# Loading x of the fourth batch at the start into a fourth buffer, instead of after slot 0 into the first batch's buffer

## The chip, the cores and the metric

The kernel runs on one core of one Trainium2 chip, which has eight. The core has five engines that work through instruction streams of their own: TensorE (PE; its weight loads are listed as PEld), VectorE (DVE), ScalarE (ACT), GpSimd (POOL) and SyncE (SP). Here SP issues nearly all plain transfers, POOL the indirect ones (gathers and scatters of rows by a list of indices), and sixteen DMA engines move the bytes. The metric is the device time of one execution in microseconds (us); lower is better. All inputs and outputs lie in the chip's HBM, in float32.

## What is computed

A small attention with a state of 32 rows per head comes first, and its output goes through two mixture-of-experts layers with the best expert per token (the first has a capacity per expert).

```python
# x (4, 8, 512, 64), state (4, 8, 32, 64): batch, head, token or state row, width
a     = softmax(x @ state^T / 8);   xread = a  @ state     # over the 32 state rows
a2    = softmax(state @ x^T / 8);   sread = a2 @ x         # over the 512 tokens
t     = concat([xread, sread], tokens)                     # 2304 rows of 512
for w_gate, w1, w2, capacity in (layer 0, layer 1):        # 8 experts, 512 -> 1024 -> 512
    e, gate = argmax, softmax value of t @ w_gate
    t = gate * (relu(t @ w1[e]) @ w2[e])                   # layer 0: rows over capacity give 0
```

## The kernel before, in words

The order of instructions on every engine is written out by hand (a manual schedule); only the semaphores decide when each starts. Each engine works strictly in that order.

**Attention.** The four batches are four "slots" (`slot(b)`, L850). One batch of x is a tile `xb` of 128 partitions by 8 heads, 4 token groups and 64 columns, 1 MiB in all (8 KiB per partition). `xload(b, n)` (L714) takes a buffer of the tag `xb` and issues the load in n pieces on SP's queue. The tag has three buffers, so batch 3 takes the buffer of batch 0. Batches 0, 1 and 2 are loaded at the start (L721 to L723); batch 3 is loaded at the end of slot 0, through the list `late` that `slot` runs last (L914, L974).

Slot b works on three batches at a time. For batch b+2 it turns x (`front_T`, L768: eight PE transposes `pt<-ident,xb` at L775 for the first half, eight for the second, each copied by ACT into `xt`), and makes the scores (`front_S`, L784). For batch b+1 it does both softmaxes (`soft_max`, `soft_exp1`, `soft_exp2`, `soft_sum1`, `soft_end`; DVE, ACT and POOL). For batch b it makes the reads: `av` (L859, tile `pav`, stored to the HBM tensor `xrows` by SP at L861) and the state's reads `sr` (L868, `pt<-xb,e2n`, the last use of that batch's `xb`; DVE takes it over at L869 as `ysr`). On PE a slot runs: `back_T` (L847), `av(0)`, `front_T` first half, `av(2)`, `sr`, `av(1)`, `front_T` second half, the state rows' turn (L588), `av(3)`, and so on. In slot 1, `front_T` reads batch 3.

**Routing beside it.** From slot 1 on, `tick` places pieces of the routing of finished batches between the others: DVE works out each token's expert (L281 to L376), PE adds up counts (L629, L630 with `upper` and `ones`, from the tile `rs` that DVE writes at L618 to L624), and `enlist` builds the experts' row lists (L333, L335 on DVE, L341 on PE). In slot 1 the counts of batch 0 give the expert with which the first layer starts (`popular`); SP then loads its weights (`load_first`, L703 and L270, tile `raw`), and POOL gathers its first 512 rows (`gather_early`, L559, into `ysb`).

**Layers.** After slot 3, PE turns the gathered rows (L1012) and the first layer begins (L1045 for the first product, L1055 for the second, in three passes of split float32). Stages of up to 512 rows of one expert follow until the end.

The three lines that decide where x of batch 3 goes and when it is loaded are

```python
t = ap_.tile([P, H, R, D], F32, tag="xb", name="xb", bufs=3)          # L715
for f in late: f()                                                    # L914, end of slot(b)
slot(0, TICKS[0], steps(0), late=(lambda: xload(3, 2),))              # L974
```

Of the kernel before, what the change touches and what calls it, by code (L numbers as in the profile page):

```python
# [10 lines left out]
F32 = mybir.dt.float32  # L11
# [9 lines left out]
P = 128  # L21
B, H, S, D = 4, 8, 512, 64
# [6 lines left out]
R = S // P  # L29
# [25 lines left out]
TICKS = ((0, 0, 0, 0, 0, 0, 0), (4, 4, 4, 4, 4, 4, 4), (6, 6, 6, 6, 6, 6, 6), (4, 4, 4, 4, 4, 4, 4))  # L55
# [22 lines left out]
def moe_kernel(ctx: ExitStack, tc: tile.TileContext, x, state, wg1, w1a, w2a, cap, wg2, w1b, w2b, out):  # L78
# [21 lines left out]
    def bc(ap, shape):  # L100
        return ap.to_broadcast(shape)
# [5 lines left out]
    def tick(n=1):  # L107
        clock[0] += 1
        while n > 0 and bgq:
            try:  # L110
                if next(bgq[0]) is PAUSE:
                    break
                n -= 1
            except StopIteration:
                bgq.popleft()
# [592 lines left out]
    with ExitStack() as ac:  # L708
        ap_ = ac.enter_context(tc.tile_pool(name="attn", bufs=1))
# [2 lines left out]
        xb_ = {}  # L712

        def xload(b, n):  # L714
            t = ap_.tile([P, H, R, D], F32, tag="xb", name="xb", bufs=3)  # L715
            k = H // n
            for a in range(n):
                SP.dma_start(out=t[:, a * k:(a + 1) * k], in_=x[b, a * k:(a + 1) * k].rearrange("h (p r) d -> p h r d", p=P))
            xb_[b] = t

        xload(0, 4)  # L721
        xload(1, 2)
        xload(2, 2)  # L723
        SP.dma_start(out=cap_i, in_=bc(cap.bitcast(I32).rearrange("(o c) -> o c", o=1), [P, 2]))
        SP.dma_start(out=wg2q[:, :, 0:E], in_=wg2.rearrange("(c p) e -> p c e", p=P))

        sd = ap_.tile([P, B, NH, P], F32, name="sd")
        vg = ap_.tile([P, B, NH, GW], F32, name="vg")
# [4 lines left out]
        def pt():  # L733

            if banks:
                banks.rotate(-1)
                return banks[0]()
            return ps.tile([P, 512], F32, tag="pt", name="pt", bufs=2)
# [29 lines left out]
        def front_T(n, i):  # L768

            if i == 0:  # L770
                xt_[n] = ap_.tile([P, H, 2, P], F32, tag="xt", name="xt")
            p = pt()
            for j in range(2):
                for q in range(2):
                    PE.transpose(p[:, (2 * j + q) * P:(2 * j + q + 1) * P], xb_[n][:, 2 * i + j, 2 * q:2 * q + 2, :].rearrange("p r d -> p (r d)"), ident)  # L775
            ACT.copy(xt_[n][:, 2 * i:2 * i + 2].rearrange("p h q c -> p (h q c)"), p)
# [10 lines left out]
        def soft_max(n, style=0):  # L787

            nb = ap_.tile([P, NH], F32, tag="nb", name="nb")
            s2 = ap_.tile([P, NH], F32, tag="s2", name="s2")  # L790
            u = [ap_.tile([P, S // NS, NS], F32, tag=f"u{o}", name=f"u{o}") for o in range(2)]
            m1 = [ap_.tile([P, S // NS], F32, tag=f"m1{o}", name=f"m1{o}") for o in range(2)]
            e2_[n] = ap_.tile([P, NH, 2, 2 * P], F32, tag="e2T", name="e2T", bufs=2)
            e1_[n] = ap_.tile([P, 2, NH, 2, P], F32, tag="e1T", name="e1T", bufs=2)
            r2_[n] = ap_.tile([P, NH], F32, tag="r2", name="r2", bufs=2)
            sm_[n] = nb, s2, u, m1

            def col_max():
                DVE.tensor_reduce(out=nb, in_=psT.rearrange("p o (a c) -> p a o c", a=NH), axis=AX.XY, op=ALU.max)
                tick(TK[0])  # L800
                DVE.tensor_scalar(nb, nb, -0.125, None, op0=ALU.mult)

            if not style:
                col_max()
            for o in range(2):
                DVE.transpose(u[o].rearrange("p k s -> p (k s)"), psT[:, o])
                tick(TK[0])
                DVE.tensor_reduce(out=m1[o], in_=u[o], axis=AX.X, op=ALU.max)
                tick(TK[0])
                POOL.tensor_tensor(out=u[o], in0=u[o], in1=bc(m1[o][:, :, None], [P, S // NS, NS]), op=ALU.subtract)  # L810
            if style:
                col_max()

        def soft_exp2(n):
            nb, s2, u, m1 = sm_[n]
            for a in range(NH):
                ACT.activation(out=e2_[n][:, a], in_=psT[:, :, a * 256:(a + 1) * 256], func=AF.Exp, bias=nb[:, a:a + 1], scale=0.125, accum_out=s2[:, a:a + 1])

        def soft_exp1(n, o):
            nb, s2, u, m1 = sm_[n]  # L820
            ACT.activation(out=u[o], in_=u[o], func=AF.Exp, scale=0.125)

        def soft_sum1(n, o):
            nb, s2, u, m1 = sm_[n]
            DVE.tensor_reduce(out=m1[o], in_=u[o], axis=AX.X, op=ALU.add)
            tick(TK[1])
            DVE.tensor_scalar(m1[o], m1[o], 1e-9, None, op0=ALU.add)
            tick(TK[1])
            DVE.reciprocal(out=m1[o], in_=m1[o])  # L829
            POOL.tensor_tensor(out=u[o], in0=u[o], in1=bc(m1[o][:, :, None], [P, S // NS, NS]), op=ALU.mult)  # L830
# [11 lines left out]
        def back_T(b, e2n, q):  # L842

            p = pt()
            for r in range(2):
                for a in range(NH):
                    PE.transpose(p[:, r * 256 + a * P:r * 256 + (a + 1) * P], e2_[b][:, a, r, q // 2 * P:(q // 2 + 1) * P], ident)  # L847
            ACT.copy(e2n[:, q:q + 2, :].rearrange("p r c -> p (r c)"), p)

        def slot(b, ticks, work=None, late=()):  # L850

            n, m = b + 1, b + 2
            nn, mm = n < B, m < B

            def av(r):

                pv = psT if not nn and r in (1, 2) else pav
                for a in range(NH):
                    PE.matmul(pv[:, a, 0:GW], e1_[b][:, r % 2, a, r // 2], vg[:, b, a], start=True, stop=True)  # L859
                ACT.copy(xr[:, r], pv[:, :, 0:GW])  # L860
                SP.dma_start(out=xrows[b * ST:b * ST + S, 0:DM].rearrange("(p r) (a w) -> p r a w", p=P, a=NH)[:, r], in_=xr[:, r, :, 0:HH * D])  # L861

            def sr():
                psr = pt()
                for a in range(NH):
                    for q in range(R):
                        for h in range(HH):
                            PE.matmul(psr[NS * h:NS * (h + 1), a * D:(a + 1) * D], e2n[:, q, a * P + NS * h:a * P + NS * (h + 1)], xb_[b][:, a * HH + h, q, :], start=(q == 0), stop=(q == R - 1))  # L868
                DVE.tensor_tensor(out=ysr[b % 2].rearrange("p (a d) -> p a d", a=NH), in0=psr[:, 0:NH * D].rearrange("p (a d) -> p a d", a=NH), in1=bc(r2_[b][:, :, None], [P, NH, D]), op=ALU.mult)  # L869

            def beside(i):
                for f in (work or {}).get(i, ()):
                    f()
                tick(ticks[i])

            e2n = ap_.tile([P, R, NH * P], F32, tag="e2n", name="e2n")
            if nn:
                soft_max(n, 1)
            back_T(b, e2n, 0)
            back_T(b, e2n, 2)  # L880
            beside(0)
            av(0)
            if mm:
                front_T(m, 0)
                front_T(m, 1)
            beside(1)
            av(2)
            if nn:
                soft_exp1(n, 0)
                soft_exp1(n, 1)  # L890
                soft_exp2(n)
            sr()
            beside(2)
            if nn:
                soft_sum1(n, 0)
            av(1)
            if mm:
                front_T(m, 2)
                front_T(m, 3)
            beside(3)  # L900
            if nn:
                soft_sum1(n, 1)
                soft_sum2(n)
            av(3)
            DVE.tensor_tensor(out=lgs[:, b, 0:R], in0=xr[:, :, 0, HH * D:GW], in1=xr[:, :, 1, HH * D:GW], op=ALU.add)
            beside(4)
            if nn:
                soft_end(n, 0)
                soft_end(n, 1)
            beside(5)  # L910
            if mm:
                front_S(m)
            beside(6)
            for f in late:  # L914
                f()

        warm(WARM)
        with tc.tile_pool(name="start", bufs=1, space=bass.MemoryType.PSUM) as sp:
# [45 lines left out]
        def steps(b, *more):  # L964

            w = {}
            for i, f in tuple(zip(READ, reads[b])) + more:
                w.setdefault(i, []).append(f)
            return w
# [1 line left out]
        def more(b):  # L971
            return tuple((i, lambda c=c: wsplit(0, c)) for c, (k, i) in enumerate(SPLIT0) if k == b)

        slot(0, TICKS[0], steps(0), late=(lambda: xload(3, 2),))  # L974
        bgq += [route(0, 1, chain(popular(rp, 0), load_first(0, (0,)))), set_apart(rp, 0), enlist_batch(0)]
        slot(1, TICKS[1], steps(1))
        bgq += [early_list(rp, 0), named("early", gather_early()), load_first(0, (1,)), route(1, 1)]
# [575 lines left out]
```

## Time and profile before

| | |
|---|---|
| time, median of 3 runs | 474.64 us (471.83 to 475.17) |
| the profiled execution | 473.61 us, of which the span from first to last instruction is 471.8 us |
| PE busy in the span | 425.9 us (90%) |
| DVE, ACT, POOL busy | 187.6, 165.4, 199.6 us (40%, 35%, 42%) |
| moved by DMA | 89.19 MB, 189 GB/s on average |
| mean granted TensorE clock | 0.975 of full speed |

The profiled execution is 1.03 us below the median of the three timed runs. Attention fills roughly the first 80 us of the span, where all engines take turns; after that PE is busy nearly without a break. A share of the whole span therefore says little about a change in the attention part: there the waits in a stretch of a few microseconds count, and whether what they delay reaches PE's long stretch behind them.

### The profile page before, as it was taken

To read this page: it belongs to the slowest core of one execution; us is meant where nothing else is said; L and a number is where in the kernel's file an instruction comes from. 1 tells how busy PE (TensorE), PEld (TensorE's weight loads), DVE (VectorE), ACT (ScalarE), POOL (GpSimd) and SP (SyncE) were. 2 spreads that over 40 slices of the span, in tenths; PEclk is the share of its full clock that TensorE was granted. 3 is DMA by queue.
4 is the path that set the end of the run, shared out by engine and by line. 5 is a ranking of instruction groups with operands and counts; after the bars stand their busy time and mean duration, and the time that the engine had idled before them with its cause. 6 is when DMAs were issued, how large, how long until landed. Compare 5 with 4: busy or idle time off the path is not lost. (4 is left out here: it accounts for less than half of the span.)

```text
span 471.8 us, 8130 instructions
## 1 busy us (share of the span) xinstructions
PE 425.9 (90%) x2757; PEld 308.2 (65%) x2757; DVE 187.6 (40%) x655; ACT 165.4 (35%) x288; POOL 199.6 (42%) x175
## 2 busy tenths in 40 slices
PE   7869577969999989999998899999989999999991
PEld 5647365757874775685775587778746856758780
DVE  7985755797140243141164141971420101411011
ACT  3757355220244421335521346203522213452110
POOL 6441264221704527305344435558443404777003
PEclk9998879998999999999999999999999999999997
DMA  7262739994999976907933300119998858210002
GB/s 234 85 167 92 222 97 297 230 172 176 394 360 385 385 268 175 363 4 253 384 126 110 85 18 2 50 53 329 399 357 262 296 178 284 91 59 22 8 0 90
DMA packets 47335, 89.19 MB, mean 189 GB/s; under 512 B 8593, under 2 KB 21137, under 8 KB 47249
## 3 DMA queue, kind: packets, MB, share of 16 engines
q1 hardware_dynamic: 42128, 72.43, 46.2%
q0 software_dynamic: 5120, 15.76, 9.9%
q8 instruction: 36, 0.59, 0.6%
q14 instruction: 51, 0.41, 0.3%
HBM read 67.70 MB, written 21.52 MB: 189 GB/s over the span
## 5 line engine op out<-in xcount | busy, mean ns | idle before, releaser
L1037 DVE SCALAR_TENSOR_TENSOR hTl<-ph,hTh 128x512 fp32r<-128x512 f32 x48 | 33.2, 691 | 204.1 <-ACT hTh L1036 196.7
L1055 PE MATMUL py<-w1h,hTh 128*128 128x512 f32 x192 | 81.6, 425 | 0.0
L275 POOL TENSOR_TENSOR w1l<-raw,w1h 128x1024 fp32r<-128x1024 f32 x22 | 52.6, 2395 | 61.9 <-ACT w1h L274 61.8
L1036 ACT ACTIVATE hTh<-ph 128x512 fp32r<-128x512 f32 x48 | 28.8, 599 | 136.8 <-PE ph L1045 82.9
L1055 PE MATMUL py<-w1h,hTl 128*128 128x512 f32 x192 | 75.7, 394 | 0.9 <-issue 0.9
L1055 PE MATMUL py<-w1l,hTh 128*128 128x512 f32 x192 | 75.5, 393 | 0.0
L1265 POOL TENSOR_TENSOR w0l<-raw,w0h 128x512 fp32r<-128x512 f32 x40 | 51.0, 1290 | 38.3 <-ACT w0h L1264 36.4
L1045 PE MATMUL ph<-xTh,w0h 128*128 128x512 f32 x192 | 54.7, 407 | 3.5 <-ACTq L1458 1.6
L1045 PE MATMUL ph<-xTl,w0h 128*128 128x512 f32 x192 | 55.4, 410 | 0.0
L1045 PE MATMUL ph<-xTh,w0l 128*128 128x512 f32 x192 | 54.8, 407 | 0.0
L1045 PEld LDWEIGHTS ph<-xTh,w0h 128*128 128x128 f32 x192 | 35.8, 191 | 13.1 <-issue 2.1
L1045 PEld LDWEIGHTS ph<-xTl,w0h 128*128 128x128 f32 x192 | 35.2, 188 | 13.4 <-issue 6.1
L1055 PEld LDWEIGHTS py<-w1h,hTh 128*128 128x128 f32 x192 | 36.1, 188 | 11.0 <-issue 4.5
L1045 PEld LDWEIGHTS ph<-xTh,w0l 128*128 128x128 f32 x192 | 35.3, 191 | 9.9 <-issue 2.5
L1055 PEld LDWEIGHTS py<-w1h,hTl 128*128 128x128 f32 x192 | 36.0, 188 | 8.2
L1073 POOL DMA_INDIRECT out_dram<-ysb,dsti x15 | 15.0, 999 | 61.6 <-ACT ysb L1063 53.6
L1055 PEld LDWEIGHTS py<-w1l,hTh 128*128 128x128 f32 x192 | 36.2, 189 | 6.6 <-issue 1.0
L1073 POOL DMA_INDIRECT yrows<-ysb,dsti x16 | 16.1, 1005 | 25.4 <-DVE oc L333 8.1
L1264 ACT CAST w0h<-raw 128x512 fp32r<-128x512 f32 x40 | 23.8, 617 | 5.1 <-DMA raw<-in_moe_w_dram 3.8
L274 ACT CAST w1h<-raw 128x1024 fp32r<-128x1024 f32 x24 | 25.1, 1044 | 0.0
L859 PE MATMUL pav<-vg,e1T 128*128 128x264 f32 x56 | 18.4, 458 | 0.5 <-ACT xr L860 0.5
L830 POOL TENSOR_TENSOR u<-u,m 128x512 f32<-128x512 f32 x8 | 8.4, 1053 | 20.7 <-DVE m L829 9.4
(314 smaller groups left out, 593.7 us busy)
## 6 DMA issues: line engine op xcount, KB each, us to landing
raw<-in_moe_w_dram SPq DMA_DIRECT2D x104, 512.0 KB, 8.2
out_dram<-zb SPq DMA_DIRECT2D x2, 2176.0 KB
xrows<-xr SPq DMA_DIRECT2D x16, 256.0 KB, 3.8
yrows<-zeros SPq DMA_DIRECT2D x3, 1026.0 KB
xb<-in_x_dram SPq DMA_DIRECT2D x6, 512.0 KB
yrows<-zeros SPq DMA_DIRECT2D x1, 1282.5 KB
xb<-in_x_dram SPq DMA_DIRECT2D x4, 256.0 KB, 4.5
st<-in_state_dram SPq DMA_DIRECT2D x1, 256.0 KB
```

The source lines that it names most:

```text
L274: ACT.copy(h, t)
L275: (POOL if on[c] else DVE).tensor_tensor(out=l, in0=t, in1=h.bitcast(F32), op=ALU.subtract)
L830: POOL.tensor_tensor(out=u[o], in0=u[o], in1=bc(m1[o][:, :, None], [P, S // NS, NS]), op=ALU.mult)
L859: PE.matmul(pv[:, a, 0:GW], e1_[b][:, r % 2, a, r // 2], vg[:, b, a], start=True, stop=True)
L1036: ACT.activation(out=hTh[:, c % 2], in_=p, func=AF.Relu)
L1037: DVE.scalar_tensor_tensor(out=hTl[:, c % 2], in0=p, scalar=0.0, in1=hTh[:, c % 2].bitcast(F32), op0=ALU.max, op1=ALU.subtract)
L1045: PE.matmul(p, w[k][:, 0, c * P:(c + 1) * P], u[:, k], start=(i == 0 and k == 0), stop=(i == 2 and k == NC1 - 1))
L1055: PE.matmul(py[t], u[:, c % 2, t * P:(t + 1) * P], w[c // 2][:, c % 2], start=(c == 0 and i == 0), stop=(c == NC2 - 1 and i == 2))
L1073: i = POOL.indirect_dma_start(out=(yrows if L == 0 else out)[:, :], out_offset=bass.IndirectOffsetOnAxis(ap=dsti[:, y:y + 1], axis=0), in_ ...
L1264: ACT.copy(h, t)
L1265: (POOL if ON[half][c] else DVE).tensor_tensor(out=l, in0=t, in1=h.bitcast(F32), op=ALU.subtract)
```

## The change

The tag `xb` gets a fourth buffer, and the load of batch 3 is issued with the others at the start, behind the two small loads `cap_i` and `wg2q`. The list `late` of `slot` goes. Every other instruction stays, in its order; lines behind L725 move by one or two in the numbering. The tiles that follow `xb` in the attention's pool lie 8 KiB per partition higher.

```diff
         def xload(b, n):
-            t = ap_.tile([P, H, R, D], F32, tag="xb", name="xb", bufs=3)
+            t = ap_.tile([P, H, R, D], F32, tag="xb", name="xb", bufs=4)
             k = H // n
             for a in range(n):
                 SP.dma_start(out=t[:, a * k:(a + 1) * k], in_=x[b, ...])
...
         xload(2, 2)
         SP.dma_start(out=cap_i, ...)
         SP.dma_start(out=wg2q[:, :, 0:E], ...)
+        xload(3, 2)
...
-        def slot(b, ticks, work=None, late=()):
+        def slot(b, ticks, work=None):
...
             beside(6)
-            for f in late:
-                f()
...
-        slot(0, TICKS[0], steps(0), late=(lambda: xload(3, 2),))
+        slot(0, TICKS[0], steps(0))
```

SP's stream is the only one in which a row moves. Before, from the first load of x to the first load of weights (`xr` is the tile of `av`'s results, `xs` that of the state's reads; x4 behind a row counts equal instructions that follow one another):

```order
L718 DMA xb<-in_x_dram 128x2x256 x4
L718 DMA xb<-in_x_dram 128x4x256 x4
L724 DMA cap_i<-in_moe_capacity_dram 128x2
L725 DMA wg2q<-in_moe_w_gate_dram 128x4x8
L861 DMA xrows<-xr 128x2x256 x3
L590 DMA xrows<-xs 32x512
L861 DMA xrows<-xr 128x2x256
L718 DMA xb<-in_x_dram 128x4x256 x2
L861 DMA xrows<-xr 128x2x256 x3
L590 DMA xrows<-xs 32x512
L861 DMA xrows<-xr 128x2x256
L703 TENSOR_LOAD efirst_135
```

The same stretch of SP's stream in the changed kernel:

```order
L718 DMA xb<-in_x_dram 128x2x256 x4
L718 DMA xb<-in_x_dram 128x4x256 x4
L724 DMA cap_i<-in_moe_capacity_dram 128x2
L725 DMA wg2q<-in_moe_w_gate_dram 128x4x8
L718 DMA xb<-in_x_dram 128x4x256 x2
L862 DMA xrows<-xr 128x2x256 x3
L590 DMA xrows<-xs 32x512
L862 DMA xrows<-xr 128x2x256 x4
L590 DMA xrows<-xs 32x512
L862 DMA xrows<-xr 128x2x256
L703 TENSOR_LOAD efirst_135
```

The two loads of batch 3 (512 KiB each) stand ahead of all five transfers of slot 0 instead of behind them. They no longer wait for PE (the last read of batch 0); each waits only for the transfer eight places before it, whose semaphore it takes over: the third and the fourth piece of batch 0.

## Rows read from the trace of the kernel before

**Rows 1.** Page, section 1: busy us (share of span), instructions.
```profile
PE 425.9 (90%) x2757; PEld 308.2 (65%) x2757; DVE 187.6 (40%) x655; ACT 165.4 (35%) x288; POOL 199.6 (42%) x175
```

**Rows 2.** Timeline of PE, slot 1: start us, duration us, instructions [idle before <-releaser].
```profile
30.93 1.06 PE L859 MATMUL pav<-vg,e1T 128*128 128x264 f32 x4
34.99 1.46 PE L775 MATMUL pt<-ident,xb 128*128 128x128 f32 x8 [3.00 <-DMA xb<-in_x_dram]
36.24 1.97 PE L859 MATMUL pav<-vg,e1T 128*128 128x264 f32 x4
38.14 1.45 PE L868 MATMUL pt<-xb,e2n 128*32 128x64 f32 x64
39.52 0.18 PE L629 MATMUL pyT<-rs,upper 128*128 128x16 bf16 x1
```

**Rows 3.** Timeline of SP's queue: issues of loads and stores.
```profile
2.68 5.31 SPq L718 DMA_DIRECT2D xb<-in_x_dram  x8
...
9.39 0.37 SPq L725 DMA_DIRECT2D wg2q<-in_moe_w_gate_dram  x1
20.83 6.35 SPq L861 DMA_DIRECT2D xrows<-xr  x3
...
29.19 1.07 SPq L718 DMA_DIRECT2D xb<-in_x_dram  x2
...
45.61 1.98 SPq L270 DMA_DIRECT2D raw<-in_moe_w_dram  x4
```

**Rows 4.** Waits in 28 to 48 us: engine, line, waited for: total us, times, longest.
```profile
DVE ysr L869 <- PE pt L868: 4.0, 1, 4.0
...
PE pt L775 <- DMA xb<-in_x_dram: 3.0, 1, 3.0
```

**Rows 5.** Stretches: length; busy us of PE, PEld, DVE, ACT, POOL; PEclk; DMA share; GB/s.
```profile
0.00:4.00 4.00, 2.66 (x10) 1.49 (x11) 1.35 (x9) 1.28 (x1) 1.84 (x13) 1.00 0.44 76
4.00:8.00 4.00, 3.18 (x24) 2.51 (x21) 3.86 (x10) 2.15 (x4) 3.99 (x10) 1.00 0.85 264
8.00:11.00 3.00, 2.50 (x40) 1.43 (x41) 2.40 (x10) 1.17 (x2) 1.93 (x4) 1.00 1.07 367
11.00:14.00 3.00, 3.00 (x87) 2.59 (x84) 2.79 (x5) 2.25 (x6) 1.05 (x2) 1.00 1.02 332
14.00:20.00 6.00, 4.45 (x56) 3.04 (x55) 5.36 (x14) 3.58 (x9) 3.15 (x3) 1.00 0.03 4
...
32.00:35.00 3.00, 0.01 (x1) 0.04 (x1) 2.96 (x10) 0.60 (x1) 1.70 (x2) 1.00 1.07 276
35.00:39.00 4.00, 4.00 (x48) 3.12 (x52) 0.60 (x5) 1.93 (x4) 0.00 (x0) 0.57 0.24 84
...
63.00:69.00 6.00, 5.46 (x26) 4.85 (x27) 3.02 (x12) 2.76 (x7) 4.70 (x3) 0.50 0.13 29
...
81.00:100.00 19.00, 18.55 (x87) 14.79 (x88) 15.58 (x65) 5.06 (x8) 3.19 (x2) 1.00 1.01 229
...
110.00:460.00 350.00, 338.19 (x1881) 242.01 (x1881) 103.29 (x341) 113.75 (x188) 155.08 (x117) 1.00 0.56 198
```

**Rows 6.** Timeline of PE, the same steps in slot 0.
```profile
19.95 1.04 PE L775 MATMUL pt<-ident,xb 128*128 128x128 f32 x8
20.86 1.16 PE L859 MATMUL pav<-vg,e1T 128*128 128x264 f32 x4
21.94 1.10 PE L868 MATMUL pt<-xb,e2n 128*32 128x64 f32 x64
```

**Rows 7.** Timeline of DVE, slot 1.
```profile
35.54 0.16 DVE L624 TENSOR_TENSOR rs<-cs,oh 128x8 bf16<-128x8 bf16 x1
39.66 0.29 DVE L869 TENSOR_TENSOR ysr<-pt,r 128x128 f32<-128x128 f32 x1 [3.96 <-PE pt L868]
```

**Rows 8.** Timeline of PE, slot 2 to the first layer.
```profile
53.04 0.37 PE L341 MATMUL listp<-lov,loc 128*96 128x128 f16 x2 [5.72 <-DVE lov L335]
...
79.65 0.66 PE L1012 MATMUL py<-ident,ysb 128*128 128x128 f32 x4 [0.72 <-DMA ysb<-xrows,gidxe]
81.08 1.17 PE L1045 MATMUL ph<-xTh,w0h 128*128 128x512 f32 x4 [0.77 <-ACT xTh L1020]
```

**Rows 9.** Timeline of POOL: the early gather.
```profile
66.31 1.21 POOL L559 DMA_INDIRECT ysb<-xrows,gidxe  x1 [0.69 <-DVE elu L392]
```

## The prediction

> **What bounds the kernel now.** I read the page's first section first: PE is busy for 425.9 us of 471.8 [rows 1]. The stretches then show two parts. From 110 to 460 us PE works 338.19 of 350 us [rows 5], so what happens there is PE's own pace; before 81 us PE starts and stops. A change to the attention can therefore only move the start of the long part, L1045 at 81.08 us [rows 8]. It pays what it takes off the chain that leads there, and no more.
>
> Next the timeline of PE in slot 1, where batch 3 is first read. `av(0)` ends at 30.93 + 1.06 = 31.99 us; the next instruction, the transposes of batch 3, starts at 34.99, and the row names the load of x as what ended 3.00 us of idleness [rows 2]. The table of waits has the same 3.0 us once, and beside it DVE waiting 4.0 us for PE's `sr` [rows 4]. SP's queue says why the data is late: the load was issued at 29.19 us [rows 3], behind the stores of slot 0, and so PE got its first half 34.99 - 29.19 = 5.8 us later. The wait has a second price. In 32 to 35 us PE did nothing; in 35 to 39 us it was granted 0.57 of its clock [rows 5], that is the lower level, 1.2 GHz, for most of the stretch. The same three steps (eight transposes, `av(2)`, `sr`) took from 34.99 to 38.14 + 1.45 = 39.59, 4.60 us [rows 2]; in slot 0, at 2.4 GHz, they took from 19.95 to 21.94 + 1.10 = 23.04, 3.09 us [rows 6]. The late load thus costs PE 3.0 + 1.5 = 4.5 us.
>
> **What the change takes off.** With the data there, the transposes start at 32.0 and `sr` ends at 32.0 + 3.09 = 35.1 us. PE cannot keep all of the 4.5 us. Its next matmul, the counts at L629, needs `rs`, which DVE finishes at 35.54 + 0.16 = 35.70 [rows 7]; DVE is busy for 2.96 of the 3 us before 35 [rows 5], with work that doesn't hang on the load. So L629 moves from 39.52 [rows 2] to about 35.75: 3.77 us. DVE goes on with `ysr` (L869) at 35.70 instead of 39.66 [rows 7]: 3.96 us. What is late next is therefore DVE's routing and softmax of slot 1, and both engines are released 3.8 to 4.0 us earlier. I take the smaller, **3.8 us**.
>
> **Whether that reaches the end.** Behind that point each milestone waits for something that has moved too: PE's long wait in slot 2 ends with DVE's lists (5.72 us before 53.04 [rows 8]), which DVE builds in the chain that starts with L869; the weight load at 45.61 [rows 3] follows a store of slot 1 and DVE's choice of an expert; the gather at 66.31 follows DVE [rows 9]; the last wait for a transfer ahead of the first layer is that for the gathered rows, 0.72 us before 79.65 [rows 8]. Nothing in these rows keeps its place in time, so I carry the 3.8 us through whole.
>
> **What the change adds.** Two issues on SP, taken from 29.19 us (1.07 us for both [rows 3]) to behind `wg2q`, which ends at 9.39 + 0.37 = 9.76. SP has nothing to issue from there until 20.83 [rows 3], so the 1.1 us are covered by 11 us of idle queue; without that cover the stores of slot 0 would be 1.1 us later, and nothing here waits for those. Each new issue waits for the third and fourth piece of batch 0, which were in place when PE used them in 8 to 11 us. The bytes: by 11.0 us the DMA engines had moved 4 x 76 + 4 x 264 + 3 x 367 GB/s x us = 2.46 MB [rows 5], and batches 0 and 1, the state and the gates are 2 x 1.05 + 0.26 + 0.03 = 2.39 MB. So batch 1 was complete by about 11 us although batch 2 stood in the queue from 8 us on: the loads are served nearly in order, and batch 3 behind batch 2 costs batch 1 nothing. Were it served alongside, batch 1 would come late by at most the 3 us that 1.05 MB take at about 350 GB/s; this is the far bound, and the sum would fall to 0.8 us. I take nothing, since batch 2 did not delay batch 1 either. Batch 3 itself then moves in 14 to 17 us, into a stretch that has 4 GB/s now [rows 5], and is read at 32: 15 us of cover; without it the 3.0 us are back. The moved addresses add no instruction. The transfer no longer runs in 30 to 35 us, beside the stores of slot 1; I count no gain for that.
>
> **The sum.** 473.61 - 3.8 = **469.8 us** for the profiled execution. The median of the three runs, 474.64, lies 1.0 us above it, and the span between the runs is 3.3 us, nearly as much as the gain.
>
> **The clock.** The part that I can place least is the half speed. In an execution where the clock did not fall after the wait, `sr` would have ended at 34.99 + 3.09 = 38.1 us, and the gain would be 38.1 - 35.7 = 2.4 us. On the other side, later half-speed stretches may come out differently: in 63 to 69 us PE worked 5.46 us at 0.50 [rows 5], worth up to 2.7 us if that stretch vanished. The Trainium skill (TensorE: Matmul & The Clock Gate, "The HAM clock gate") says that the window by which the gate judges runs freely and doesn't start with the kernel. By that rule a shift of 3.8 us alone can move, lengthen or remove a half-speed stretch, which gives the cases of less and of more gain below; the trace shows one placement, after an idle PE, and cannot show the spread.
>
> **The rivals.**
> 1. *Less*: the clock would mostly not have fallen, or the join at 79.65 gives part back. For: the three runs differ by 3.3 us. Against: three fully idle us ahead of the fall. Time: 473.61 - 2.4 = 471.2 us.
> 2. *More*: a later half-speed stretch shortens as well. 469.8 - 2.7 = 467.1 us. For: they stand behind waits of similar length that have moved; against: these waits keep their length.
> 3. *Nothing*: the path to 81 us isn't the one through DVE, and the wait for the rows [rows 8] grows by what was won. 473.6 us. Against: the gather is issued behind DVE's list [rows 9], which moves.
> 4. *Slower*: the first layer begins at the lower clock. In 81 to 100 us PE is busy 18.55 of 19 us at 1.00 [rows 5]; each us there at half speed costs 0.5 us. The turn of the rows ahead of it leaves PE partly idle, so the clock could fall there. It decides from 7.6 us on (3.8 / 0.5); the longest such stretch seen is the 6 us of [rows 5], and 10 us would give 469.8 + 5 = 474.8 us. Against: now the clock is full through it.
>
> **Chances.** The full shift (469 to 471) 0.55, less 0.18, more 0.12, nothing 0.09, slower 0.06. The range 467.0 to 472.8 us holds the first three; it leaves out the last two and a tail below. About 1% (4.7 us) is what a measurement of this kernel can tell from no change. The forecast of 3.8 us is 0.8%, just inside it, so: faster by over 1% 0.29 (the "more" case and the upper third of the full one), within 1% 0.67, slower 0.04.
>
> **What would show it.** SP issues x of batch 3 at about 9.8 us, and the stretch 14 to 17 us carries some 350 GB/s. PE's transposes in slot 1 start at 32.0 with no wait for a load, at granted clock 1.00; `ysr` (one line number higher) starts at about 35.7 with no 4 us of idleness. The first layer's L1045 starts at about 81.08 - 3.8 = 77.3 us, and the rest keeps its length. I am wrong if the transposes move and 77.3 doesn't come: then the row that waits in slots 2 or 3 names the step that failed. I am wrong in the other direction if batch 1's transposes at 11 us now wait for their load.

## The result, and the profile after

The changed kernel takes 470.50 us (median of 20 runs, 467.59 to 475.37), the kernel before 474.61 (20 runs, 471.83 to 476.96). The ratio is 0.9912 with a 95% interval of 0.9891 to 0.9934: 4.2 us less, between 3.1 and 5.2. Forecast were 469.8 us for the profiled execution and a gain of 3.8. Ratios in this document are estimated from fast runs alone (one run of the changed kernel, 475.37 us, counts as slow), and a difference taken from a ratio can lie up to 1.5 us from that of the two medians.

The profiled execution of the changed kernel took 473.97 us, 3.5 us more than its median and no less than the one of before (473.61). It shows the mechanism, and also how a gain is lost again in one execution. PE's share on the page:

```profile
PE 430.0 (91%) x2757; PEld 312.5 (66%) x2757; DVE 188.3 (40%) x655; ACT 165.6 (35%) x288; POOL 199.5 (42%) x175
```

SP's queue (start, duration, instructions), against [rows 3]:

```profile
7.67 2.42 SPq L724 DMA_DIRECT2D cap_i<-in_moe_capacity_dram  x1
...
10.61 2.45 SPq L718 DMA_DIRECT2D xb<-in_x_dram  x2
...
41.87 1.99 SPq L270 DMA_DIRECT2D raw<-in_moe_w_dram  x4
```

Batch 3 is issued at 10.61 us instead of 29.19, and the first weights at 41.87 instead of 45.61. PE in slot 1 and further on, against [rows 2, 8] (the numbers of lines behind the attention are one lower):

```profile
31.85 1.04 PE L776 MATMUL pt<-ident,xb 128*128 128x128 f32 x8
32.72 1.14 PE L860 MATMUL pav<-vg,e1T 128*128 128x264 f32 x4
33.79 1.10 PE L869 MATMUL pt<-xb,e2n 128*32 128x64 f32 x64
35.78 0.17 PE L629 MATMUL pyT<-rs,upper 128*128 128x16 bf16 x1 [0.90 <-DVE rs L624]
...
49.20 0.37 PE L341 MATMUL listp<-lov,loc 128*96 128x128 f16 x2 [5.63 <-DVE lov L335]
...
51.37 1.94 PE L869 MATMUL pt<-xb,e2n 128*32 128x64 f32 x64
...
74.65 0.82 PE L1011 MATMUL py<-ident,ysb 128*128 128x128 f32 x4 [0.91 <-DMA ysb<-xrows,gidxe]
77.16 1.11 PE L1011 MATMUL py<-ident,ysb 128*128 128x128 f32 x4 [1.69 <-DMA ysb<-xrows,gidxe]
79.04 2.05 PE L1044 MATMUL ph<-xTh,w0h 128*128 128x512 f32 x4 [0.77 <-ACT xTh L1019]
```

The transposes of batch 3 follow `av(0)` without a wait, at full clock; the next wait is the one for `rs`, 0.90 us. Up to the lists of slot 2 the gain is whole: 53.04 - 49.20 = 3.84 us. After that it melts in this execution. DVE's rows of slot 1, against [rows 7], and of slot 2:

```profile
35.57 0.16 DVE L624 TENSOR_TENSOR rs<-cs,oh 128x8 bf16<-128x8 bf16 x1
35.65 0.28 DVE L870 TENSOR_TENSOR ysr<-pt,r 128x128 f32<-128x128 f32 x1
...
53.37 0.29 DVE L870 TENSOR_TENSOR ysr<-pt,r 128x128 f32<-128x128 f32 x1 [2.63 <-PE pt L869]
```

The same step of slot 2 in the kernel before:

```profile
56.73 0.29 DVE L869 TENSOR_TENSOR ysr<-pt,r 128x128 f32<-128x128 f32 x1 [2.15 <-PE pt L868]
```

And the early gather on POOL, against [rows 9]:

```profile
63.40 1.21 POOL L559 DMA_INDIRECT ysb<-xrows,gidxe  x1 [0.52 <-DVE elu L392]
```

Behind the lists of slot 2 DVE waited 0.48 us longer for `sr` than before, and the gather was issued 2.91 us earlier, not 3.84.

The stretches (length; busy us of PE, PEld, DVE, ACT, POOL; granted clock; DMA share; GB/s) show where it goes:

```profile
14.00:17.00 3.00, 2.16 (x52) 1.34 (x42) 2.86 (x7) 2.96 (x8) 1.54 (x2) 1.00 0.99 328
32.00:35.00 3.00, 2.89 (x77) 2.36 (x75) 2.97 (x10) 2.68 (x6) 1.73 (x2) 1.00 0.26 92
35.00:39.00 4.00, 3.22 (x23) 2.67 (x23) 3.50 (x20) 3.54 (x10) 0.75 (x1) 1.00 0.31 105
...
47.00:53.00 6.00, 3.80 (x70) 3.07 (x70) 3.71 (x17) 1.48 (x3) 0.97 (x1) 0.56 0.73 238
...
74.00:80.00 6.00, 2.89 (x10) 1.97 (x11) 3.23 (x11) 2.61 (x5) 3.04 (x4) 0.58 1.06 348
80.00:86.00 6.00, 6.00 (x17) 4.67 (x16) 2.89 (x12) 0.60 (x1) 0.00 (x0) 0.56 0.84 161
```

The last two stretches in the kernel before:

```profile
74.00:80.00 6.00, 3.84 (x34) 3.15 (x34) 3.05 (x16) 4.13 (x9) 1.97 (x1) 1.00 1.03 369
80.00:86.00 6.00, 5.23 (x24) 4.11 (x23) 5.23 (x22) 2.13 (x3) 1.80 (x4) 1.00 0.84 163
```

In 32 to 39 us the clock is now 1.00 (before: 0.57 from 35 on [rows 5]). From 74 to 86 us it is under 0.6, where the kernel before had 1.00. So this execution reached the first product only 2.0 us earlier (79.04 against 81.08) and ran the first of it at 1.2 GHz.

### The profile page after: what moved, and what is told of

It is laid out like the page before. It is cut to its first block, busy times and chain, and to the rows that moved or that the text cites. A ratio compares the mean times of both kernels' runs of the same rounds, so it can differ in the third digit from the quotient of the medians.

```text
span 472.2 us, 8128 instructions
## 1 busy us (share of the span) xinstructions
PE 430.0 (91%) x2757; PEld 312.5 (66%) x2757; DVE 188.3 (40%) x655; ACT 165.6 (35%) x288; POOL 199.5 (42%) x175
## 5 line engine op out<-in xcount | busy, mean ns | idle before, releaser
L1035 ACT ACTIVATE hTh<-ph 128x512 fp32r<-128x512 f32 x48 | 28.8, 599 | 139.5 <-PE ph L1044 95.8
L1264 POOL TENSOR_TENSOR w0l<-raw,w0h 128x512 fp32r<-128x512 f32 x40 | 50.9, 1292 | 36.8 <-ACT w0h L1263 34.9
L1044 PE MATMUL ph<-xTh,w0h 128*128 128x512 f32 x192 | 56.9, 420 | 3.3 <-ACTq L1457 1.5
L1044 PE MATMUL ph<-xTl,w0h 128*128 128x512 f32 x192 | 56.4, 415 | 0.0
L1044 PE MATMUL ph<-xTh,w0l 128*128 128x512 f32 x192 | 56.2, 416 | 0.0
L1044 PEld LDWEIGHTS ph<-xTh,w0h 128*128 128x128 f32 x192 | 37.3, 199 | 13.6 <-issue 3.2
L1054 PEld LDWEIGHTS py<-w1h,hTh 128*128 128x128 f32 x192 | 36.2, 189 | 10.3 <-issue 3.9
L1203 PE MATMUL pyT<-raw,xTf 128*32 128x256 f32 (+1 forms) x144 | 16.8, 454 | 0.0
```

Of the source, the lines that this page charges most:

```text
L1035: ACT.activation(out=hTh[:, c % 2], in_=p, func=AF.Relu)
L1044: PE.matmul(p, w[k][:, 0, c * P:(c + 1) * P], u[:, k], start=(i == 0 and k == 0), stop=(i == 2 and k == NC1 - 1))
L1054: PE.matmul(py[t], u[:, c % 2, t * P:(t + 1) * P], w[c // 2][:, c % 2], start=(c == 0 and i == 0), stop=(c == NC2 - 1 and i == 2))
L1203: PE.matmul(pyv[q * n:(q + 1) * n, 0:w], xTf[:, c, 0:n], w1[c][:, 0, q * w:(q + 1) * w], start=(c == 0), stop=(c == NC1 - 1))
L1264: (POOL if ON[half][c] else DVE).tensor_tensor(out=l, in0=t, in1=h.bitcast(F32), op=ALU.subtract)
```

## The experiments

**The two halves of the change.** The fourth buffer alone, and the earlier load alone. The buffer alone:

```diff
-t = ap_.tile([P, H, R, D], F32, tag="xb", name="xb", bufs=3)
+t = ap_.tile([P, H, R, D], F32, tag="xb", name="xb", bufs=4)
```

> One half of the change alone: the tag xb gets its fourth buffer, but the load of batch 3 stays where it was, at the end of slot 0, behind the five stores of slot 0 on SP's queue. Theory (what held the load back was its place in SP's order; the buffer of batch 0 had been free since sr ended at 23.04 us, 6 us before the load was issued): nothing changes, 474.6 us within 1 us; x of batch 3 is still issued at about 29 us, PE still waits about 3.0 us in slot 1, and the clock still falls to 1.2 GHz after it. Rival (the load waited for the buffer): the load is issued earlier and the time falls by some 4 us to 470.5.

Measured: 476.50 us beside 474.91, ratio 1.0030 (1.0000 to 1.0059). The issue of the load on SP, the wait on PE, and the clock behind the wait:

```profile
29.38 2.59 SPq L718 DMA_DIRECT2D xb<-in_x_dram  x2
```

```profile
35.15 1.06 PE L775 MATMUL pt<-ident,xb 128*128 128x128 f32 x8 [2.93 <-DMA xb<-in_x_dram]
...
37.03 1.10 PE L868 MATMUL pt<-xb,e2n 128*32 128x64 f32 x64
```

```profile
35.00:39.00 4.00, 3.85 (x82) 3.29 (x83) 1.51 (x10) 2.94 (x6) 0.00 (x0) 1.00 0.37 128
```

The buffer wins nothing (by the ratio 1.4 us more, a little beyond the 1 us that was allowed): the load is issued at 29.38 us, where it was before, and the wait is as long. This profile shows something else, which was not expected: behind the same idle stretch the clock did not fall this time. `sr` ended at 38.13 us, not 39.59, so the late load cost 1.46 us less in this execution than in the first.

The load alone, into the buffer of batch 0, placed behind `sr(0)`:

```diff
             sr()
+            if b == 0:
+                xload(3, 2)
             beside(2)
...
-slot(0, TICKS[0], steps(0), late=(lambda: xload(3, 2),))
+slot(0, TICKS[0], steps(0))
```

> The other half without the buffer: three buffers as before, the load of batch 3 still into the buffer of batch 0, but issued in slot 0 right behind sr(0), that is behind two stores instead of five. Theory (place in the queue): the issue follows sr's end at about 23.1 us, lands by about 28 to 29, PE transposes batch 3 at 32.0 without a wait, and the time is that of the full change, 470.5 us within 1 us. Rival (the early load is needed, or the stores that now queue behind the load delay slot 1): 472 us or more, with a wait in slots 0 or 1 that the changed kernel doesn't have.

Measured: 471.61 us beside 474.91, ratio 0.9924 (0.9891 to 0.9957). SP's load and PE:

```profile
23.31 1.03 SPq L718 DMA_DIRECT2D xb<-in_x_dram  x2
```

```profile
32.05 1.04 PE L775 MATMUL pt<-ident,xb 128*128 128x128 f32 x8
```

The gain of the change, within the noise, without its buffer: what counted was the place in SP's order.

**A larger dose.** The load one store later, in slot 1 behind `av(0)`:

```diff
             av(0)
+            if b == 1:
+                xload(3, 2)
             if mm:
```

> A larger dose: three buffers, and the load of batch 3 one store later than before, behind the first store of slot 1, so it is issued at about 33.0 us instead of 29.2. Theory (each us by which the load is late behind 23 to 28 us reaches the end): PE's wait grows from 3.0 to about 6.8 us, the time rises by 3.5 to 4 us to about 478.3. Rival (slots 2 and 3 have slack that takes up a delay of this size): 474.6 to 476 us.

Measured: 479.75 us beside 474.91, ratio 1.0105 (1.0069 to 1.0141), 5.0 us more by the ratio, where 3.5 to 4 were expected. PE's wait grew to 5.48 us (6.8 were expected), at half clock behind it, and the lists of slot 2 came 3.83 us later than in [rows 8]:

```profile
37.86 1.94 PE L775 MATMUL pt<-ident,xb 128*128 128x128 f32 x8 [5.48 <-DMA xb<-in_x_dram]
...
56.87 0.37 PE L341 MATMUL listp<-lov,loc 128*96 128x128 f16 x2 [5.69 <-DVE lov L335]
...
85.17 1.17 PE L1047 MATMUL ph<-xTh,w0h 128*128 128x512 f32 x4 [0.77 <-ACT xTh L1022]
```

Lateness of this load reaches the end of the kernel, in both directions.

**The clock by itself.** Idle matmuls in the wait of the kernel before; first 16 more of them:

```diff
             av(0)
+            if b == 1:
+                warm(16)
             if mm:
```

> The kernel before with its late load, plus 16 idle matmuls (128x336 bf16 of zeros into a bank nobody reads then, about 0.157 us each, 2.5 us) on PE between av(0) and the transposes of batch 3 in slot 1, inside the 3.0 us wait. It separates the two prices of the wait. Theory (the wait costs 3.0 us, and the half clock behind it another 1.5): the wait for the load ends at about the same time, 35.0 us, the clock in 35 to 39 us stays at 2.4 GHz, sr ends at 38.1 instead of 39.6, and the time falls by 1.4 us to about 473.2. Rival (the half clock costs nothing here since another engine is the bound): 474.6 us.

Measured: 484.53 us beside 474.91, ratio 1.0223 (1.0185 to 1.0261). Slot 1 did what was expected, but PE lost far more later on:

```profile
35.56 1.06 PE L775 MATMUL pt<-ident,xb 128*128 128x128 f32 x8 [1.04 <-DMA xb<-in_x_dram]
...
37.45 1.10 PE L868 MATMUL pt<-xb,e2n 128*32 128x64 f32 x64
...
198.30 2.05 PE L1047 MATMUL ph<-xTh,w0h 128*128 128x512 f32 x4 [4.74 <-issue]
...
457.08 1.17 PE L1047 MATMUL ph<-xTh,w0h 128*128 128x512 f32 x4 [2.81 <-PEq L1460]
```

At 198 and 457 us PE stands for 4.74 and 2.81 us and waits for no engine and no transfer; in the kernel before, the second of these is 0.70 us. So this run leaves the theory untested. The extra instructions were suspected, and the next experiment kept their number: eight idle matmuls in the wait, and fewer but wider ones at the start.

```diff
-WARM, WARM2, WARM3, WARM4, STYLE, WN = (13, 2, 12, 0, 1, 336)
+WARM, WARM2, WARM3, WARM4, STYLE, WN = (9, 2, 8, 0, 1, 512)
...
             av(0)
+            if b == 1:
+                warm(8)
```

> The kernel before with its late load and eight idle matmuls of 128x512 bf16 (1.7 us) in the 3.0 us wait of slot 1, the idle matmuls at the start cut from 27 of 336 columns to 19 of 512, so that PE has as many instructions as before. With 16 more instructions pairs on PE the time had risen by 9.6 us although slot 1 was 1.1 us quicker: a 4.7 us stall of PE behind a branch near 195 us, where it waited for nothing that the trace shows. Theory (that stall came from the moved code, and the clock behind the wait is worth up to 1.2 us in the executions in which it falls): no such stall, sr of slot 1 at 2.4 GHz, 473.5 to 474.6 us. Rival (idle matmuls here cost time by themselves): above 476 us.

Measured: 474.57 us beside 475.89, ratio 0.9973 (0.9939 to 1.0007). No such stall; the transposes run at full clock behind a shorter wait:

```profile
34.74 1.07 PE L775 MATMUL pt<-ident,xb 128*128 128x128 f32 x8 [1.33 <-DMA xb<-in_x_dram]
```

In slot 1 the clock behind the wait is worth what the prediction gave it (1.5 us): from the start of the transposes to the end of `sr` it took 2.99 us here, and 4.60 before. In the time it isn't shown: 1.3 us less by the medians, and the interval just takes in no difference. The 473.5 to 474.6 us that were expected were met, beside a kernel before that took 1 us more in this job than in the last.

**Is the first profile typical?** The changed kernel twice more, unchanged.

> The changed kernel as it is, for another profile. Its first profile showed 3.8 us won at the end of slot 1 and all of it gone at the first layer: the last gathered rows came 2.5 us earlier instead of 3.8, and the first layer began at 1.2 GHz for some 6 us. Theory (that was the accident of one execution, since that one took 473.97 us against a median of 470.5): in an execution near the median L1044 starts at about 77.3 us at granted clock 1.00, and the first product after it keeps the 3.8 us. Rival (the change itself brings the rows late and the clock down): the same waits for the gathered rows, 2.6 us, and the same half clock at 79 us again.

> The changed kernel a third time, for the comparison with the two above and for a third profile. Theory (slot 1 is 3.8 us quicker in every execution where the clock fell after the late load, 2.3 to 2.6 where it did not; what reaches the first product depends on where the later half-clock stretches fall): lists of slot 2 at 49.2 to 49.4 us, first product between 77 and 80 us, time 3 to 4.5 us below the kernel before. Rival (the shift is rigid): first product at 77.3 us.

Measured: 472.13 us beside 475.89, ratio 0.9932 (0.9898 to 0.9966); and 469.67 beside 472.73, ratio 0.9934 (0.9903 to 0.9965). Of their profiles, the turn of the gathered rows in the one, and the first product in both:

```profile
75.33 3.50 PE L1011 MATMUL py<-ident,ysb 128*128 128x128 f32 x16
79.60 1.17 PE L1044 MATMUL ph<-xTh,w0h 128*128 128x512 f32 x4 [0.77 <-ACT xTh L1019]
```

```profile
49.46 0.37 PE L341 MATMUL listp<-lov,loc 128*96 128x128 f16 x2 [5.62 <-DVE lov L335]
...
78.19 1.17 PE L1044 MATMUL ph<-xTh,w0h 128*128 128x512 f32 x4 [0.77 <-POOL ysb L1496]
```

Of the second profile neither theory holds whole. PE does not wait for the rows there, and the first product runs at full clock. But 77.3 us isn't reached: 79.60, and 78.19 in the third, which falls where that run's theory had it. The turn of the rows fell into a half-clock stretch (3.50 us for what took 1.53 + 0.66 in the kernel before). And in slot 3 of the second profile PE stood three times within `sr` and waited for nothing that the profile shows:

```profile
PE pt L869 <- issue: 1.3, 3, 0.5
```

The buffer alone and the load alone have the same 1.3 and 1.4 us, the kernel before 0.3, the first and the third profile none. From the lists of slot 2 to the first product it took 28.0, 30.2 and 28.3 us in the profiles with the late load (before, buffer alone, larger dose), and 29.8, 30.3, 28.7 and 30.2 us with the early one (first, second and third profile, load alone).

**The gathered rows.** In the first profile they seemed to be held up by the 2 MB of weights that were issued ahead of the last gather; so the weights were moved behind.

```diff
-bgq += [early_list(rp, 0), named("early", gather_early()), load_first(0, (1,)), route(1, 1)]
+bgq += [early_list(rp, 0), named("early", gather_early()), idle(1), route(1, 1)]
...
-slot(3, TICKS[3], steps(3, *more(3)))
+slot(3, TICKS[3], steps(3, *more(3), (5, lambda: list(load_first(0, (1,))))))
```

> The changed kernel with the load of the first expert's second weights (four pieces of 512 KiB) moved in SP's order from behind the first store of slot 3 (issued at 66.94 us) to behind the third store of slot 3, about 3 to 4 us later; everything else in its order. The fourth gather was issued at 67.96, behind that load, and landed after 8.4 us where the shortest took 3.5. Theory (the gathered rows are late because 2 MB of weights share the DMA engines with them): the rows land at about 72.5, PE turns them without a wait, L1044 starts 2 us earlier or more than in the same execution with the early load, and the time falls by 1 to 3 us to 468 to 469.5, as the weights are first read at about 79 us. Rival (the gathers are slow by themselves, or the weights are then late): same time as the changed kernel, 470.5, or a wait for raw of up to 3 us instead, 473.

Measured: 473.79 us beside 475.89, ratio 0.9961 (0.9928 to 0.9993), against 0.9932 of the changed kernel in the same job. The weights were issued at 74.67 us instead of 66.94, twice as far behind as was meant. PE had no wait for the rows, but neither had the changed kernel there; ACT now waited for the weights:

```profile
ACT w1h L274 <- DMA raw<-in_moe_w_dram: 1.2, 1, 1.2
```

Taking the weights away won nothing. But the rows were not late in the profile beside it, and the new wait may hide a gain, so what held up the rows in the first profile stays open.

**The next half-clock stretch.** Every profile with PE idle for 5.6 to 5.7 us ahead of the lists of slot 2 has the lower clock behind it. First, eight idle matmuls near the end of that wait, in the changed kernel, with the same number of instructions:

```diff
-WARM, WARM2, WARM3, WARM4, STYLE, WN = (13, 2, 12, 0, 1, 336)
+WARM, WARM2, WARM3, WARM4, STYLE, WN = (9, 2, 8, 0, 1, 512)
...
             av(0)
+            if b == 2:
+                PE.matmul(pyv[:, 0:S // NS], zb[:, 0:P], sm_[n][3][1].bitcast(BF16)[:, 1::2], start=True, stop=True)
+                warm(7)
```

> The changed kernel with eight idle matmuls in slot 2, in the 5.6 us in which PE waits for DVE's lists: one small one that waits for a row maximum of DVE's softmax, about 2.4 us before the lists, and seven of 128x512 bf16 behind it (0.216 us each, 1.5 us). The idle matmuls at the start are cut from 27 of 336 columns to 19 of 512, so that PE's instruction count stays. Theory (the half clock behind that wait costs slot 2 time: av(2) took 2.07 us instead of 1.16, sr 1.94 instead of 1.10, and DVE then waits 2.6 us for sr): granted clock stays at 1.00 in 49 to 53 us, and the time falls by about 1.5 us to 469. Rival (the half clock is not on the path there, or the idle matmuls are too few to hold it): 470.5 us.

> The kernel of the eight idle matmuls in slot 2 once more, beside the changed kernel in the same job. It was 469.60 us there against 472.13 for the changed kernel, from six runs, with intervals that overlap, and its profile had the clock at 0.50 in slot 2 all the same. Theory (that gain was partly the spread of the executions): between 0 and 2.5 us below the changed kernel. Rival (it is a gain of its own): again 2 us or more below it, with intervals apart.

Measured: 469.60 us beside 475.89, ratio 0.9875 (0.9821 to 0.9930); the second time 467.97 beside 472.73, ratio 0.9907 (0.9874 to 0.9941). In the first profile the clock fell all the same and the idle matmuls themselves ran slowly, in the second it held:

```profile
46.84 2.77 PE L249 MATMUL pyT<-zb 128*128 128x512 bf16 x6 [0.23 <-issue]
```

```profile
47.40 1.46 PE L249 MATMUL pyT<-zb 128*128 128x512 bf16 x6
```

Against the changed kernel in the same jobs that is 2.5 and 1.7 us less, with intervals that overlap. So most of the wait was filled, with five float32 matmuls of about 0.9 us (two instructions each in the rows):

```diff
-WARM, WARM2, WARM3, WARM4, STYLE, WN = (13, 2, 12, 0, 1, 336)
+WARM, WARM2, WARM3, WARM4, STYLE, WN = (8, 2, 7, 0, 1, 512)
...
             av(0)
+            if b == 2:
+                z = zb.bitcast(F32)
+                for _ in range(5):
+                    PE.matmul(pyv, z[:, 0:P], bc(z[:, None, :], [P, 2, 2 * P]), start=True, stop=True)
```

> The changed kernel with five idle float32 matmuls (128x512, about 1 us each) between av(0) and the first list matmul of slot 2, so that PE works through most of the 5.6 us in which it waits for DVE's lists, and not only at the end of it; idle matmuls at the start cut from 27 of 336 columns to 17 of 512. In every profile so far the clock fell to 1.2 GHz behind that wait and stayed there for 3 to 6.6 us. Theory (the half clock follows from the idle PE and delays sr of slot 2, for which DVE waits 2.6 us): granted clock 1.00 through 49 to 55 us, sr of slot 2 at 1.10 us instead of 1.94, the gather's first issue at about 62.3 us instead of 63.7, time 1.5 us below the changed kernel in the same job. Rival (later half-clock stretches move and take it back): the slot is quicker and the first product starts no earlier.

> The kernel with five idle float32 matmuls in slot 2 once more, in a job of its own, for a second ratio to the kernel before. The changed kernel's three ratios were 0.9912, 0.9932 and 0.9934; this one's first was 0.9897. Theory (the idle matmuls are worth 1.5 us and more): a ratio at or under 0.990, and a spread of its runs of 2 to 3 us, since one of the half-clock stretches is gone. Rival (the first result was luck): 0.992 to 0.993.

Measured: 467.28 us (465.90 to 467.97) beside 472.73, ratio 0.9897 (0.9869 to 0.9925); the second time 467.35 beside 472.85, ratio 0.9853 (0.9810 to 0.9896). The first profile, PE and then DVE and the stretch:

```profile
43.64 4.46 PE L887 MATMUL pyT<-zb 128*128 128x512 f32 x10
49.42 0.27 PE L341 MATMUL listp<-lov,loc 128*96 128x128 f16 x2 [1.32 <-DVE lov L335]
...
50.57 1.10 PE L869 MATMUL pt<-xb,e2n 128*32 128x64 f32 x64
...
76.19 2.05 PE L1048 MATMUL ph<-xTh,w0h 128*128 128x512 f32 x4 [0.77 <-ACT xTh L1023]
```

```profile
51.73 0.29 DVE L870 TENSOR_TENSOR ysr<-pt,r 128x128 f32<-128x128 f32 x1 [0.78 <-PE pt L869]
```

```profile
47.00:53.00 6.00, 4.68 (x82) 2.98 (x81) 5.08 (x22) 2.28 (x6) 1.05 (x1) 1.00 0.80 275
```

The first product in the second profile:

```profile
75.32 1.17 PE L1048 MATMUL ph<-xTh,w0h 128*128 128x512 f32 x4 [0.77 <-ACT xTh L1023]
```

`sr` of slot 2 takes 1.10 us instead of 1.94, DVE waits 0.78 us for it (in the three profiles of the changed kernel 2.63 each time), and the first product starts at 76.19 us. The shorter start is not what did it: the lists came at 49.42 us, beside 49.46 in the changed kernel of the same job. By the medians this version takes 2.4 us less than the changed kernel in that job (the spread of the two sets of runs gives 1.3 to 3.6), and in both jobs about 5.5 us less than the kernel before (by the ratios 4.9 and 6.9). In the first profile the first product began at the lower clock, in the second at the full one. That second execution reached its second product 2.4 us earlier, at 81.00 us instead of 83.41, but took only 0.6 us less (466.57 against 467.16), so what the full clock there is worth isn't shown. In both profiles PE waits for the gathered rows again (2.0 and 1.7 us), so they are the next limit of the turn.

## Why the prediction was right, point by point

- **The bound.** Right. The wait for batch 3 on PE was the price: the load alone won it back, and the larger dose made it larger.
- **What is taken off.** Right in each number of slot 1. `sr` was forecast to end at 35.1 and ended at 34.9; L629 was forecast at 35.75 and came at 35.78, behind the wait for `rs` that was named as the next; `ysr` at 35.70, it came at 35.65. The lists of slot 2 came 3.84 us earlier; 3.8 were carried.
- **What is added.** Nearly right. The issues came at 10.6 us (10.0 and 10.3 in the other profiles) instead of 9.8 and took 2.45 us instead of 1.07, still under the cover, and batch 3 moved in 14 to 17 us at 328 GB/s where 350 were forecast. The prediction's sign of batch 1 losing to it did show in the first profile, where its turn waited 0.22 + 0.27 us for its load. But the other two profiles have no such wait, and the load alone, with batch 3 not issued before 23.31 us, has one of 0.33 + 0.38; so the early load is not its cause. It cost nothing: the next product of slot 0 started at 17.11 us, as before at 17.10.
- **Whether it reaches the end whole.** This step was too simple. 77.3 us for the first product was not met in any of three profiles (79.04, 79.60, 78.19). The row that the prediction asked for is DVE's wait for `sr` in slot 2: the half clock behind the lists lasted longer than in the profile of before, so that this wait was 2.63 us in all three and not 2.15, and the `av` behind `sr` took 1.52 and 1.77 us in two of them and not 1.11. Of 3.6 to 3.8 us at the lists, 2.6 to 3.1 were left at the gather. The buffer alone, with its late load, has the 2.62 us too, so it is not the early load as such. The experiment that filled the wait took this part away. Further on, the way to the first product depends on the rows, on the half-clock stretches and on PE's stands in slot 3; from the lists it takes 28 to 30 us in all.
- **The sum.** Rivals 3 and 4 of the prediction, the rows that come late and the first layer that begins at the lower clock, both happened in the first profile; in the timed runs they did not carry the day. Three comparisons of the same two kernels gave 0.9912, 0.9932 and 0.9934, that is 4.2, 3.2 and 3.1 us: the sum of 3.8 lies among them, and each one's interval holds it. But the profiles show only 2.0, 1.5 and 2.9 us of it at the first product, and the profiled execution, for which 469.8 us was forecast, took 473.97. Nor does the rest keep its length: from the second product to the end it took 385.1 us before and 384.7, 386.8 and 383.9 in the changed kernel. So the total came out as summed by steps that did not all hold, and that it came so near is in part luck. Whether the early load lengthens the way behind the lists a little on average (29.8 us in four profiles against 28.8 in three; with the other runs that have the 5.6 us wait unfilled, 29.9 in five against 28.8 in five) is left open; single executions can't settle a difference of 1 us there.
- **What can be told apart.** Too careful. The prediction held 1% to be the least difference from no change that can be seen; the interval of the 20 runs is 0.2% either way, and 0.9% stands clear of it.
- **The clock.** The two bounds were right for slot 1: with the fall 3.8 us, without it 2.4. The profile of the buffer alone had the wait without the fall; its lists came at 51.57 us, and 51.57 - 49.20 = 2.4. The Trainium skill (TensorE: Matmul & The Clock Gate, "The HAM clock gate") says that the gate's window runs freely and doesn't start anew with the kernel; the two profiles with an idle stretch of 2.9 and 3.0 us at the same place, one with a fall and one without, agree with that, though they don't show the window itself.
- **Not asked and found.** The fourth buffer isn't needed. The load alone, three stores (5.9 us) earlier in SP's order and into the old buffer, gives the same gain within the noise (0.9924).

## What to carry to other kernels

A load whose buffer is free may still be late because of what stands ahead of it in its issuing engine's order; compare the time of issue with the time when the buffer's last reader ends before spending memory on another buffer. Price a wait on TensorE by two sums, with and without the lower clock behind it, and take the next engine's ready time as the limit of the gain. And compare milestones in several profiles before carrying a shift through to the end: one execution can hide a gain that the timed runs have, and a half-clock stretch behind a later wait can take back part of a shift.

## What the runs showed of the hardware

- Sixteen additional small matmuls with their weight loads in slot 1, at 32 us, cost 9.6 us by the medians. Two stands of PE, 4.74 and 2.81 us, came some 165 and 425 us later, with no engine and no transfer to wait for; they don't make up the whole. With the number of instructions kept, eight idle matmuls cost nothing measurable. That the moved code is the cause was not tried by itself.
- The clock falls behind an idle PE in some executions and not in others, at the same place: 1.00 or 0.57 in 35 to 39 us behind 3 us of idleness. Behind 5.6 us of idleness it was at 0.50 (49 to 53 us) in all three profiles of the changed kernel; with five idle matmuls of 4.46 us in that gap it stayed at 1.00 in both profiles. With eight idle matmuls at the end of the gap it held in one profile and fell in the other.
